# Attention and SwiGLU on one core: the first batch in groups of 128, 256 and 384 queries

## The chip, the cores and the metric

The kernel runs on one core of one Trainium2 chip. The metric is device time in microseconds of one execution, input loads and output stores included. TensorE (PE in the profile) multiplies matrices and turns tiles; VectorE (DVE) and ScalarE (ACT) work on elements; GpSimd (POOL) issues the loads that cast from float32 to bfloat16 and computes one small power for each group; SyncE (SP) issues the other DMAs. Each engine takes its instructions in the order of the program and waits for others through semaphores.

## The reference

Sparse attention over 4 batches, 8 heads, 768 positions and head dimension 64, then, over the 3072 rows of 512, a root-mean-square normalisation and a feed-forward block with gate:

```python
scores = scale * np.matmul(q, k.transpose(0, 1, 3, 2))
scores = np.where(mask, scores, -1e9)   # 32-wide blocks: neighbours, first, last, three sampled
attn = softmax(scores)
x = (attn @ v) as rows of H * D = 512
xn = x / np.sqrt(np.mean(x * x, axis=-1) + 1e-6) * rms_g
g, val = xn @ w_gate, xn @ w_val        # 512 -> 1536
out = (g * sigmoid(g) * val) @ w_out    # 1536 -> 512
```

## The kernel before

The work goes in groups of queries of one batch. `groups` (L51) holds three groups of 256 queries for batch 0 and two of 384 for each of the other three batches, nine in all. The main loop (L545) goes over the groups and inside over the eight heads. For a head, `scores` multiplies K (stationary, 128 keys at a time) with the group's queries into a PSUM tile `st` and ACT takes the exponential into `ex` (768 elements a partition in one instruction); the mask is carried by 24 extra rows of `KT` and `QT` below the 64 of the head, so that K, Q and mask are one product. One head later `pv` multiplies `ex` with V into the PSUM tile `op` (one buffer), and VectorE normalises it into `stage`.

The feed-forward of a group runs inside the attention of the next one. After the last head's `pv`, `after_pv` sums the squares on VectorE, POOL raises them to -0.5 (`rms_power`, L330, the tile `rstd`), VectorE scales the rows (`rms_scale`, the tile `xs`), and x is turned into `xg`: by TensorE and VectorE for the first two groups and the last (`transpose_x`), by a DMA transpose on SP for the others (`by_dma`, L335). At head `tx` of the next group `enter` (L438) puts the feed-forward's pieces into the list `fill`: a gate and a value product for each of 12 column blocks, then four parts of the down product for each 128 queries. `position` (L443) is called four times a head and emits pieces at the rate set by `enter`. So the order on each engine is written out by the loop, while the places of buffers in a pool are chosen when the program is built.

K and Q must be turned so that the head dimension lies on partitions. Batch 0's are turned by TensorE (`first_turn`, `transpose_qk`) and copied to `KT` and `QT` while the first group runs; the later batches' are turned by DMA transposes on SP (`turn`) and placed by further DMAs (`place`). `keep_busy` issues matmuls on zeros that nobody reads, in the first group (`thin`).

POOL issues in this order: the loads of batch 0 (K, Q and V by pairs of heads), the first half of the columns of the gate and value weights (`load_gv(0)`), in the first group's second head the other half and the down weights `wo`, then the first group's power, then in the second group K, Q and V of batch 1 for pairs 0 and 1, `gain`, K and Q of pairs 2 and 3, then the second group's power. Eight semaphores serve the loads in turn, so a load waits until the eighth one ahead of it has landed. SP issues, among others, the copies of the mask rows: for batch 1's buffers (`KT[1]`, `QT[1]`, 288 KB each) in the first group's sixth head (L478).

Of the kernel before, what the change touches and what calls it, by code (L numbers as in the profile page):

```python
# [17 lines left out]
def kernel(  # L18
# [18 lines left out]
    P = 128  # L37
# [10 lines left out]
    HC = NC // 2  # L48
    TGM = HC * P

    groups = [(0, c, 2) for c in range(0, NC, 2)]  # L51
    groups += [(b, c, HC) for b in range(1, B) for c in range(0, NC, HC)]
    FIRST = NC // 2
    KR = D + NB
    NP = H // 2
    VW = D + 1
# [30 lines left out]
    wg = persist.tile([P, KD, DFF], BF16, name="wg")  # L87
    wv = persist.tile([P, KD, DFF], BF16, name="wv")
    wo = persist.tile([P, NF, DM], BF16, name="wo")
    NWC = 2  # L90
    WC = DFF // NWC

    def load_gv(j):
        for t, src in ((wg, moe_w_gate), (wv, moe_w_val)):
            nc.gpsimd.dma_start(
                out=t[:, :, j * WC:(j + 1) * WC],
                in_=src.rearrange("(c p) f -> p c f", p=P)[:, :, j * WC:(j + 1) * WC])
# [5 lines left out]
    def cast_v(b, pr, eng):  # L103
        eng.tensor_copy(  # L104
            out=Vp[b % 2][:, 2 * pr:2 * pr + 2, :, 0:D], in_=vraw.pop((b, pr)))


# [55 lines left out]
    for pr in range(NP):  # L163
        if pr + 1 < NP:
            load_qk(0, pr + 1)
        load_v(0, pr)
    load_gv(0)

    mhalf = const.tile([P, HC], FP32, name="mhalf")
    nc.vector.memset(mhalf, -0.5)  # L170
# [79 lines left out]
    def transpose_qk(pr, which, lo, hi, spare, copy):  # L250

        b = 0
        src = (kbf if which == 0 else qbf)[(b, pr)]
        dst = (KT if which == 0 else QT)[b % 2]
        pool, tag = (ps_f, "ff") if spare else (ps_o, "ot")
        t = pool.tile([P, 2, HC, P], BF16, name="tqk", tag=tag)
        for e in range(2):
            for cc in range(lo, hi):  # L260
                nc.tensor.transpose(  # L261
                    out=t[:, e, cc, :], in_=src[:, e, 2 * cc * D:(2 * cc + 2) * D],
                    identity=ident)
        view = dst[0:D, 2 * pr:2 * pr + 2, :].rearrange("p e (c w s) -> p e c w s", w=2, s=P)
        for w in range(2):
            copy(out=view[:, :, lo:hi, w, :], in_=t[w * D:(w + 1) * D, :, lo:hi])  # L266

    turned = {}

# [19 lines left out]
    def scores(grp, h, part, ex):  # L289

        b, c0, n = grp
        tg = n * P
        nj = 2 if n == HC else 3
        st = ps_s.tile([P, 1024], FP32, name="st", tag="st")
        at = st.rearrange("p (j t) -> p j t", t=512 if n == HC else tg)
        for e in range(nj):
            jt = nj * part + e
            nc.tensor.matmul(  # L298
                out=at[:, e, 0:tg], lhsT=KT[b % 2][0:KR, h, jt * P:(jt + 1) * P],
                rhs=QT[b % 2][0:KR, h, c0 * P:c0 * P + tg], start=True, stop=True)  # L300
# [32 lines left out]
        e["xg"] = work.tile([P, KD, TGM], BF16, name="xg", tag="xg", bufs=2)  # L333

    def by_dma(e):  # L335
        return e["grp"] not in (groups[0], groups[1], groups[-1])

    def rms_scale(e, it):
        if it >= e["grp"][2]:
# [121 lines left out]
    def side_work(gi, h):  # L461

        if gi == 0:
            if h == 0:
                copy_rows(KT, kind, 2, 4, 0, S)
                copy_rows(QT, qmask, 2, 4, 0, 2 * P)
            if h % 2 == 0:
                cast_v(0, h // 2, nc.vector)
            if h == 1:
                load_gv(1)  # L470
                nc.gpsimd.dma_start(out=wo, in_=moe_w_out.rearrange("(c p) f -> p c f", p=P))
            if h == 1:
                for third in range(1, FIRST):
                    mask_queries(third)
                nc.sync.dma_start(
                    out=QT[0][D:KR, 1:H, 2 * P:S],
                    in_=qmask[:, 2 * P:S].unsqueeze(1).to_broadcast([NB, H - 1, S - 2 * P]))
            if h == 5:  # L478
                for T, m in ((KT, kind), (QT, qmask)):
                    nc.sync.dma_start(out=T[1][D:KR, :, :],  # L480
                                      in_=m.unsqueeze(1).to_broadcast([NB, H, S]))
        if gi == 1:
            if h == 1:
                load_qk(1, 0)
                load_v(1, 0)
                load_v(1, 1)
                load_qk(1, 1)
            if h == 3:
                nc.gpsimd.dma_start(
                    out=gain, in_=moe_rms_g.unsqueeze(0).to_broadcast([P, DM]))  # L490
                load_qk(1, 2)
            if h == 5:
                load_qk(1, 3)

    def turn_first(gi, h):


        if gi == 0 and h == 0:
            transpose_qk(1, 0, 0, HC, True, nc.vector.tensor_copy)
        if gi == 0 and 0 < h < H - 2:  # L500
            if h % 2:
                transpose_qk(h // 2 + 1, 1, 0, 1, True,
                             nc.scalar.copy if h < 4 else nc.vector.tensor_copy)
            else:
                transpose_qk(h // 2 + 1, 0, 0, HC, True, nc.vector.tensor_copy)
        if gi == 0 and h >= H - 2:
            e = h - (H - 2)
            t = first_turn((q16, second16[1])[e], 1, HC)
            for w in range(2):
                first_copy(e, 1, t, w, 1, HC, nc.vector.tensor_copy)  # L510
        if gi == 1 and h in (0, 2, 4):
            transpose_qk(h // 2 + 1, 1, 1, HC, h == 0, nc.vector.tensor_copy)

    def casts(gi, b, g, h):


        if gi + 1 < FIRST or h not in (2, 4):
            return
        n = h // 2 - 1
        if b == 0:  # L520
            cast_v(1, n, nc.vector)
            load_v(1, 2 + n)
            return
        if g == 0:
            cast_v(b, 2 + n, nc.vector)
        elif b + 1 < B:
            cast_v(b + 1, n, nc.vector)
        if b + 1 < B:
            load_v(b + 1, 2 * g + n)
            load_qk(b + 1, 2 * g + n)  # L530
# [13 lines left out]

    for gi, grp in enumerate(groups):  # L545
        b, c0, n = grp
        g = c0 // n
        parts = 3 if n == HC else 2
        cur = {
            "stage": work.tile([P, HC, DM], BF16, name="stage", tag="stage", bufs=2),  # L550
            "ssq": work.tile([P, HC], FP32, name="ssq", tag="ssq", bufs=2),
            "grp": grp,
        }
        tx = 1 if gi == 1 else TX
        for h in range(H):
            ex = ex_tile(n)
            thin = gi == 0 or (gi == 1 and h <= tx)
            if gi == 0 and h in (1, 2):
                keep_busy(2, 512)
            scores(grp, h, 0, ex)  # L560
            if h == 0 and prev is not None and prev[0]["grp"][2] == HC:
                squares(prev[0], 2, 0, (H - 1) * D)
            if gi == 0 and h == 0:
                scores(grp, h, 1, ex)
                second = [first_turn(t16, 0, 1 if which else HC)
                          for which, t16 in enumerate(second16)]
                for which in range(2):
                    for w in range(2):
                        first_copy(1, which, second[which], w, 0, 1 if which else HC,
                                   nc.vector.tensor_copy)  # L570
                copy_rows(KT, kind, 1, 2, 0, S)
                copy_rows(QT, qmask, 1, 2, 0, 2 * P)
                nc.vector.tensor_scalar(out=rmsg, in0=rmsg, scalar1=float(DM) ** 0.5,
                                        scalar2=None, op0=ALU.mult)
            if h == 1 and ending is not None and tx > 1:
                rms_scale(ending, 1)
            if h == tx and ending is not None and tx > 1:
                transpose_x(ending, 0)
            if gi == 0 and h:
                turn_first(gi, h)  # L580
            if thin:
                keep_busy(1, 512)
            position()
            if gi or h:
                scores(grp, h, 1, ex)
            side_work(gi, h)
            position()
            if h == 1 and ending is not None and tx > 1:
                rms_scale(ending, 2)
            if thin:  # L590
                keep_busy(1, 512)
# [9 lines left out]
            if h == tx == 1 and ending is not None:  # L601
                transpose_x(ending, 0)
# [6 lines left out]
            if h == tx and ending is not None:  # L609
                transpose_x(ending, 1)  # L610
                enter(ending, NPOS + 4 * (TX - tx))
                ending = None
            if gi == 1:
                turn_first(gi, h)
            casts(gi, b, g, h)
            turns(gi, b, g, h)
            if gi == FIRST and h == 0:
                nc.vector.tensor_scalar(out=gain, in0=gain, scalar1=float(DM) ** 0.5,
                                        scalar2=None, op0=ALU.mult)
            if h == 0 and ending is not None:  # L620
                rms_scale(ending, 0)
                if tx == 1:
                    rms_scale(ending, 1)
            if h == H - 1:
                squares(cur, 1, 0, (H - 1) * D)
            prev = (cur, h, ex)
    pe, ph, pex = prev
# [50 lines left out]
```

## Time and profile before

| | |
|---|---|
| median of 3 runs (lowest, highest) | 316.9 us (315.94, 317.04) |
| the profiled execution: its time, its span | 317.69 us, 315.9 us |
| TensorE matmul busy | 305.8 us, 97% of the span |
| TensorE weight load busy | 200.5 us |
| VectorE busy | 205.5 us |
| ScalarE busy | 207.4 us |
| GpSimd busy | 47.3 us |
| DMA moved | 37.24 MB, 118 GB/s over the span |

Durations of single instructions come from one profiled execution. Matmuls overlap, so the time that one costs in a row is the distance of starts and not the mean duration in its row. A row such as "rstd waits, idle 1.58 <-DVE ssq" says how long the engine had nothing to do before the instruction and what ended that. The landing time of a DMA is counted from its issue.

### The profile page before, as it was taken

How to read it: one execution, taken by the hardware profiler on the slowest of the kernel's cores; microseconds unless marked ns; L12 is line 12 of the kernel's file. 1: busy time of each engine (PE TensorE's matmuls, PEld its weight loads, DVE VectorE, ACT ScalarE, POOL GpSimd, SP SyncE). 2: the span in 40 equal slices, each digit the busy share in tenths (PEclk: the TensorE clock that was granted, in tenths of full speed). 3: DMA queues.
4: the chain of work that ended last, by engine and by line, in shares of the span. 5: the costliest groups of instructions: out<-in, count | busy, mean ns of one | idle time of the engine just before them, and what ended most of it. 6: DMA issues, size and time to landing. Idle time of an engine off the chain costs nothing.

```text
span 315.9 us, 7285 instructions
## 1 busy us (share of the span) xinstructions
PE 305.8 (97%) x2869; PEld 200.5 (63%) x2869; DVE 205.5 (65%) x563; ACT 207.4 (66%) x336; POOL 47.3 (15%) x70
## 2 busy tenths in 40 slices
PE   8888999999899999999999999999999999989995
PEld 4566886886588556655666566655666566645653
DVE  7987875678367657682767457683767546683860
ACT  6687776677688676676766766766767666722331
POOL 9705221000220122012020122010000100010000
PEclk9999999999999999999999999999999999999999
DMA  7999999997779487705784288814000230002002
GB/s 143 297 242 212 209 247 188 162 201 131 190 134 164 86 183 152 133 20 130 160 163 100 50 192 125 152 38 118 33 2 0 48 105 2 3 0 100 2 0 101
DMA packets 66766, 37.24 MB, mean 118 GB/s; under 512 B 49532, under 2 KB 62444, under 8 KB 66732
## 3 DMA queue, kind: packets, MB, share of 16 engines
q1 hardware_dynamic: 53000, 19.59, 29.2%
q0 software_dynamic: 13696, 17.17, 28.6%
q8 instruction: 22, 0.36, 0.5%
q14 instruction: 12, 0.10, 0.1%
q10 hardware_dynamic: 36, 0.01, 0.0%
HBM read 28.59 MB, written 6.29 MB: 110 GB/s over the span
## 4 chain that ended last, share of the span: by engine, by line
PE 89%; DVE 7%; DMA 2%; ACT 1%; issue 1%; POOL 0%; DVEq 0%; ACTq 0%
PE gp L379 20%; PE vp L390 19%; PE st L298 19%; PE yp L407 18%; PE op L310 11%; DVE junk L322 2%; DMA xg<-xs 2%; PE unread L151 1%; PE tx L361 1%; DVE stage L315 1%; ACT ex L301 1%; DVE KT L208 0%; DVE u L394 0%; PE tqk L261 0%; DVE KT L266 0%
## 5 line engine op out<-in xcount | busy, mean ns | idle before, releaser
L301 ACT ACTIVATE ex<-st 128x768 bf16<-128x768 f32 x192 | 154.4, 812 | 58.1 <-PE st L298 56.0
L298 PE MATMUL st<-QT,KT 88*128 88x384 bf16 (+1 forms) x432 | 94.6, 309 | 0.8 <-ACT ex L301 0.4
L394 DVE SCALAR_TENSOR_TENSOR u<-th,gp 128x384 bf16<-128x384 bf16 (+1 forms) x108 | 54.8, 508 | 43.1 <-ACT th L383 41.5
L379 PE MATMUL gp<-xg,wg 128*128 128x384 bf16 (+1 forms) x432 | 80.4, 307 | 1.2 <-DMA xg<-xs 1.2
L390 PE MATMUL vp<-xg,wv 128*128 128x384 bf16 (+1 forms) x432 | 80.1, 307 | 0.4 <-DVE u L394 0.4
L407 PE MATMUL yp<-wo,hps 128*128 128x512 bf16 (+1 forms) x300 | 74.0, 370 | 0.7 <-DVE hps L396 0.7
L383 ACT ACTIVATE th<-gp 128x384 bf16<-128x384 f32 (+1 forms) x108 | 48.9, 453 | 28.0 <-PE gp L379 27.8
L396 DVE TENSOR_TENSOR hps<-u,vp 128x384 bf16<-128x384 bf16 (+1 forms) x108 | 55.1, 510 | 11.7 <-PE st L298 0.5
L298 PEld LDWEIGHTS <-KT 88*128 88x128 bf16 x432 | 41.6, 98 | 26.9 <-DVE QT L222 1.3
L379 PEld LDWEIGHTS <-wg 128*128 128x128 bf16 x432 | 40.2, 97 | 21.9 <-DMA xg<-xs 1.3
L390 PEld LDWEIGHTS <-wv 128*128 128x128 bf16 x432 | 40.5, 97 | 20.8 <-issue 0.8
L310 PEld LDWEIGHTS <-ex 128*128 128x128 bf16 x1152 | 46.1, 98 | 11.5 <-DVE stage L315 1.3
L310 PE MATMUL op<-Vp,ex 128*128 128x65 bf16 x1152 | 48.8, 194 | 1.1 <-DVE stage L315 0.6
L407 PEld LDWEIGHTS <-hps 128*128 128x128 bf16 x300 | 27.7, 97 | 23.7 <-DVE hps L396 1.2
L314 DVE RECIPROCAL rz<-op 128x3 f32<-128x3 f32 (+1 forms) x72 | 12.5, 173 | 29.0 <-PE op L310 28.8
L330 POOL TENSOR_TENSOR rstd<-ssq,mhalf 128x3 f32<-128x3 f32 (+1 forms) x9 | 7.3, 814 | 150.0 <-DVE ssq L322 150.0
L315 DVE TENSOR_TENSOR stage<-op,rz 128x192 bf16<-128x192 f32 (+1 forms) x72 | 24.1, 335 | 2.5
L413 ACT ACTIVATE yo<-yp 128x512 f32<-128x512 f32 (+1 forms) x25 | 14.4, 577 | 17.0 <-PE yp L407 17.0
L83 POOL DMA_DIRECT2D vraw<-in_v_dram x16 | 12.0, 748 | 70.9 <-DVE Vp L104 70.7
L322 DVE CUSTOM_DVE_ANT_0 junk<-stage 128x448 bf16<-128x448 bf16 x24 | 14.9, 623 | 0.6
L342 DVE SCALAR_TENSOR_TENSOR xs<-stage,rstd,gain 128x512 bf16<-128x512 bf16 x17 | 11.8, 748 | 4.5 <-POOL rstd L330 4.4
L151 PE MATMUL unread<-idle 128*128 128x512 bf16 (+1 forms) x37 | 12.6, 391 | 1.2 <-DVE idle L144 1.2
(61 smaller groups left out, 98.7 us busy)
## 6 DMA issues: line engine op xcount, KB each, us to landing
vraw<-in_v_dram POOLq DMA_DIRECT2D x16, 384.0 KB, 4.9
out_dram<-yo SPq DMA_DIRECT2D x23, 256.0 KB, 2.3
kbf<-in_k_dram POOLq DMA_DIRECT2D x15, 192.0 KB, 6.2
qbf<-in_q_dram POOLq DMA_DIRECT2D x15, 192.0 KB, 6.5
KT<-turned SPq DMA_DIRECT2D x24, 96.0 KB, 3.6
QT<-turned SPq DMA_DIRECT2D x24, 96.0 KB, 2.4
wg<-in_moe_w_gate_dram POOLq DMA_DIRECT2D x2, 768.0 KB, 16.4
wv<-in_moe_w_val_dram POOLq DMA_DIRECT2D x2, 768.0 KB, 20.2
```

The costliest lines, as they stand in the source:

```text
L151: nc.tensor.matmul(out=t[:, 0:cols], lhsT=idle[:, 0:P], rhs=idle[:, 0:cols], start=True, stop=True)
L298: nc.tensor.matmul(out=at[:, e, 0:tg], lhsT=KT[b % 2][0:KR, h, jt * P:(jt + 1) * P], rhs=QT[b % 2][0:KR, h, c0 * P:c0 * P + tg], start=Tru ...
L301: nc.scalar.activation(out=ex[:, nj * part:nj * (part + 1), :], in_=at[:, 0:nj, 0:tg], func=AF.Exp, scale=SCALE)
L310: nc.tensor.matmul(out=op[:, it, 0:VW], lhsT=ex[:, jt, it * P:(it + 1) * P], rhs=Vp[b % 2][:, h, jt, :], start=(jt == 0), stop=(jt == NC - 1))
L315: nc.vector.tensor_tensor(out=stage[:, 0:n, h * D:(h + 1) * D], in0=op[:, 0:n, 0:D], in1=rz[:, 0:n].unsqueeze(2).to_broadcast([P, n, D]), ...
L322: nc.vector.tensor_tensor_reduce(out=junk[:, 0:hi - lo], in0=part, in1=part, scale=1.0, scalar=(e["ssq"][:, it:it + 1] if lo else DM * 1e- ...
L379: nc.tensor.matmul(out=gp[:, 0:tg], lhsT=wg[:, c, f * P:(f + 1) * P], rhs=xg[:, c, 0:tg], start=(c == 0), stop=(c == KD - 1))
L383: nc.scalar.activation(out=th[:, 0:tg], in_=gp[:, 0:tg], func=AF.Tanh, scale=0.5)
L390: nc.tensor.matmul(out=vp[:, 0:tg], lhsT=wv[:, c, f * P:(f + 1) * P], rhs=xg[:, c, 0:tg], start=(c == 0), stop=(c == KD - 1))
L394: nc.vector.scalar_tensor_tensor(out=u[:, 0:tg], in0=th[:, 0:tg], scalar=1.0, in1=gp[:, 0:tg], op0=ALU.add, op1=ALU.mult)
L396: nc.vector.tensor_tensor(out=hps[:, f, 0:tg], in0=u[:, 0:tg], in1=vp[:, 0:tg], op=ALU.mult)
L407: nc.tensor.matmul(out=yp, lhsT=hps[:, f, tt * P:(tt + 1) * P], rhs=wo[:, f, lo:hi], start=(f == 0), stop=(f == NF - 1))
```

## The change

Batch 0 goes in groups of 128, 256 and 384 queries, in this order. The number of groups stays nine. For 128 queries one `scores` call takes all six key blocks of a head (`nj` 6), so that there is one exponential a head in the first group, two in the second, three in the third. The third group's x is turned by TensorE instead of by DMA transposes. The weights' columns are loaded as a quarter and a quarter ahead of the main loop and a half in the first group's second head; `wo` follows as before. Half of the K copies and two V casts of batch 0 go to ACT, the Q copies to VectorE. The copies of the mask rows for batch 1 are issued by POOL in the second group's sixth head, behind K and Q of the last pair, instead of by SP in the first group. The second group's x enters at the third head for all groups.

```diff
-    groups = [(0, c, 2) for c in range(0, NC, 2)]
+    groups = [(0, 0, 1), (0, 1, 2), (0, 3, HC)]
     groups += [(b, c, HC) for b in range(1, B) for c in range(0, NC, HC)]
-    FIRST = NC // 2
+    FIRST = len(groups) - 2 * (B - 1)
...
-    load_gv(0)
+    load_gv(0, NF // 4)
+    load_gv(NF // 4, NF // 2)
...
-            copy(out=view[:, :, lo:hi, w, :], in_=t[w * D:(w + 1) * D, :, lo:hi])
+            copy[w](out=view[:, :, lo:hi, w, :], in_=t[w * D:(w + 1) * D, :, lo:hi])
...
-        nj = 2 if n == HC else 3
+        nj = {1: 6, 2: 3, 3: 2}[n]
...
-        return e["grp"] not in (groups[0], groups[1], groups[-1])
+        return e["grp"] not in groups[:FIRST] and e["grp"] != groups[-1]
...
-                cast_v(0, h // 2, nc.vector)
+                cast_v(0, h // 2, nc.vector.tensor_copy if h < 4 else nc.scalar.copy)
             if h == 1:
-                load_gv(1)
+                load_gv(NF // 2, NF)
...
-                    out=QT[0][D:KR, 1:H, 2 * P:S],
-                    in_=qmask[:, 2 * P:S].unsqueeze(1).to_broadcast([NB, H - 1, S - 2 * P]))
-            if h == 5:
-                for T, m in ((KT, kind), (QT, qmask)):
-                    nc.sync.dma_start(out=T[1][D:KR, :, :],
-                                      in_=m.unsqueeze(1).to_broadcast([NB, H, S]))
+                    out=QT[0][D:KR, 1:H, HC * P:S],
+                    in_=qmask[:, HC * P:S].unsqueeze(1).to_broadcast([NB, H - 1, S - HC * P]))
+            if h == 4:
+                copy_rows(QT, qmask, 1, H, 2 * P, HC * P)
         if gi == 1:
...
             if h == 5:
                 load_qk(1, 3)
+                for T, m in ((KT, kind), (QT, qmask)):
+                    nc.gpsimd.dma_start(out=T[1][D:KR, :, :],
+                                        in_=m.unsqueeze(1).to_broadcast([NB, H, S]))
...
-        tx = 1 if gi == 1 else TX
...
-            if h == tx and ending is not None and tx > 1:
+            if h == TX and ending is not None:
                 transpose_x(ending, 0)
+                if gi == 1:
+                    transpose_x(ending, 1)
+                    enter(ending, NPOS + 4)
+                    ending = None
```

In the built program after the change, POOL's instructions from the down weights on stand in this order, with what each waits for (the pairs of heads are counted from 0):

```
wo                     waits: V of batch 0, pair 2, landed
rstd, first group      waits: VectorE's squares
K(1,0) Q(1,0) V(1,0) V(1,1) K(1,1) Q(1,1) gain
K(1,2)                 waits: wo landed
Q(1,2)                 waits: K(1,0) landed
K(1,3)                 waits: Q(1,0) landed
Q(1,3)                 waits: V(1,0) landed, and SP's turn of Q(1,0) complete
mask rows of KT[1]     waits: V(1,1) landed
mask rows of QT[1]     waits: K(1,1) landed
rstd, second group     waits: VectorE's squares
```

In the program before, Q(1,3) has the buffer of batch 0's last Q pair and waits for TensorE's reading of that one; after the change it has the buffer of Q(1,0).

More of the change, by code (lines that the diff above doesn't have):

```diff
@@ L89, with load_gv @@
     wo = persist.tile([P, NF, DM], BF16, name="wo")
-    NWC = 2
-    WC = DFF // NWC
-    def load_gv(j):
+    def load_gv(lo, hi):
         for t, src in ((wg, moe_w_gate), (wv, moe_w_val)):
             nc.gpsimd.dma_start(
-                out=t[:, :, j * WC:(j + 1) * WC],
-                in_=src.rearrange("(c p) f -> p c f", p=P)[:, :, j * WC:(j + 1) * WC])
+                out=t[:, :, lo * P:hi * P],
+                in_=src.rearrange("(c p) f -> p c f", p=P)[:, :, lo * P:hi * P])
     KT = [persist.tile([P, H, S], BF16, name=f"KT{i}") for i in range(2)]
@@ L101, with cast_v @@
     Vp = [persist.tile([P, H, NC, VW], BF16, name=f"Vp{i}") for i in range(2)]
-    def cast_v(b, pr, eng):
-        eng.tensor_copy(
+    def cast_v(b, pr, copy=nc.vector.tensor_copy):
+        copy(
             out=Vp[b % 2][:, 2 * pr:2 * pr + 2, :, 0:D], in_=vraw.pop((b, pr)))
@@ L493, in side_work @@
                 load_qk(1, 3)
+                for T, m in ((KT, kind), (QT, qmask)):
+                    nc.gpsimd.dma_start(out=T[1][D:KR, :, :],
+                                        in_=m.unsqueeze(1).to_broadcast([NB, H, S]))
     def turn_first(gi, h):
+        dve, act = nc.vector.tensor_copy, nc.scalar.copy
         if gi == 0 and h == 0:
-            transpose_qk(1, 0, 0, HC, True, nc.vector.tensor_copy)
+            transpose_qk(1, 0, 0, HC, True, (dve, act))
         if gi == 0 and 0 < h < H - 2:
             if h % 2:
-                transpose_qk(h // 2 + 1, 1, 0, 1, True,
-                             nc.scalar.copy if h < 4 else nc.vector.tensor_copy)
+                transpose_qk(h // 2 + 1, 1, 0, 1, True, (dve, dve))
             else:
-                transpose_qk(h // 2 + 1, 0, 0, HC, True, nc.vector.tensor_copy)
+                transpose_qk(h // 2 + 1, 0, 0, HC, True, (dve, act))
         if gi == 0 and h >= H - 2:
@@ L511, in turn_first @@
         if gi == 1 and h in (0, 2, 4):
[L512 removed]
+            transpose_qk(h // 2 + 1, 1, 1, HC, h == 0, (dve, dve))
     def casts(gi, b, g, h):
@@ L520, in casts @@
         if b == 0:
-            cast_v(1, n, nc.vector)
+            cast_v(1, n)
             load_v(1, 2 + n)
@@ L524, in casts @@
         if g == 0:
-            cast_v(b, 2 + n, nc.vector)
+            cast_v(b, 2 + n)
         elif b + 1 < B:
-            cast_v(b + 1, n, nc.vector)
+            cast_v(b + 1, n)
         if b + 1 < B:
@@ L546 @@
         b, c0, n = grp
-        g = c0 // n
-        parts = 3 if n == HC else 2
+        g = 0 if c0 == 0 else 1
+        parts = n
         cur = {
@@ L553 @@
         }
-        tx = 1 if gi == 1 else TX
         for h in range(H):
             ex = ex_tile(n)
-            thin = gi == 0 or (gi == 1 and h <= tx)
+            thin = gi == 0 or (gi == 1 and h <= TX)
             if gi == 0 and h in (1, 2):
@@ L563 @@
             if gi == 0 and h == 0:
-                scores(grp, h, 1, ex)
                 second = [first_turn(t16, 0, 1 if which else HC)
                           for which, t16 in enumerate(second16)]
+                copy_rows(KT, kind, 1, 2, 0, S)
+                copy_rows(QT, qmask, 1, 2, 0, 2 * P)
                 for which in range(2):
@@ L569 @@
                         first_copy(1, which, second[which], w, 0, 1 if which else HC,
[L570 to L575, printed above, removed]
+                                   nc.vector.tensor_copy if which or not w else nc.scalar.copy)
+            if h == 1 and ending is not None:
                 rms_scale(ending, 1)
-            if h == tx and ending is not None and tx > 1:
+            if h == TX and ending is not None:
                 transpose_x(ending, 0)
+                if gi == 1:
+                    transpose_x(ending, 1)
+                    enter(ending, NPOS + 4)
+                    ending = None
             if gi == 0 and h:
@@ L583 @@
             position()
-            if gi or h:
+            if parts > 1:
                 scores(grp, h, 1, ex)
@@ L587 @@
             position()
-            if h == 1 and ending is not None and tx > 1:
+            if h == 1 and ending is not None:
                 rms_scale(ending, 2)
@@ L600 @@
                 copy_rows(QT, qmask, 4, H, 0, 2 * P)
-            if h == tx == 1 and ending is not None:
-                transpose_x(ending, 0)
             position()
@@ L608 @@
             position()
-            if h == tx and ending is not None:
+            if h == TX and ending is not None:
                 transpose_x(ending, 1)
-                enter(ending, NPOS + 4 * (TX - tx))
+                enter(ending, NPOS)
                 ending = None
@@ L616 @@
             turns(gi, b, g, h)
+            if gi == 0 and h == H - 1:
+                nc.vector.tensor_scalar(out=rmsg, in0=rmsg, scalar1=float(DM) ** 0.5,
+                                        scalar2=None, op0=ALU.mult)
             if gi == FIRST and h == 0:
@@ L621 @@
                 rms_scale(ending, 0)
-                if tx == 1:
-                    rms_scale(ending, 1)
-            if h == H - 1:
+            if h == H - 1 and n > 1:
                 squares(cur, 1, 0, (H - 1) * D)
```

## The prediction

> **What bounds it now.** I read the page's busy slices first, then the chain of waits, then the timelines of POOL and SP, because the change touches what those two issue.
>
> ```profile
> PE   8888999999899999999999999999999999989995
> ...
> DMA  7999999997779487705784288814000230002002
> ```
>
> TensorE is busy from the first slice to the last, so the time is its work plus what it can't do in the first microseconds and in waits. DMA is full over the first nine slices (71 us), while the weights and two batches load.
>
> ```profile
> 27.61 0.73 POOL rstd L330
> ...
> 28.37 0.78 DVE xs L348 x2
> ...
> 81.12 2.44 DMA xg<-xs
> 83.56 0.05 issue
> 83.60 0.61 PE gp L379 x4
> ```
>
> This is the chain: after the last head of a group it goes through POOL's power (rstd), VectorE's xs and, for the third group, a DMA transpose. On TensorE's timeline that transpose leaves 0.91 us idle, not 2.44.
>
> ```profile
> 14.71 1.03 POOL L471 DMA_DIRECT2D wo<-in_moe_w_out_dram  x1
> 27.61 0.72 POOL L330 TENSOR_TENSOR rstd<-ssq,mhalf 128x2 f32<-128x2 f32 x1 [11.87 <-DVE ssq L322]
> ...
> 44.31 0.70 POOL L75 DMA_DIRECT2D kbf<-in_k_dram  x1 [6.96 <-DMA wo<-in_moe_w_out_dram]
> 45.55 0.71 POOL L75 DMA_DIRECT2D qbf<-in_q_dram  x1 [0.54 <-PE op L310]
> 46.34 0.72 POOL L75 DMA_DIRECT2D kbf<-in_k_dram  x1
> 47.54 0.71 POOL L75 DMA_DIRECT2D qbf<-in_q_dram  x1 [0.49 <-PE vp L390]
> 49.83 0.71 POOL L330 TENSOR_TENSOR rstd<-ssq,mhalf 128x2 f32<-128x2 f32 x1 [1.58 <-DVE ssq L322]
> ```
>
> POOL works in order, and each load waits until the eighth load ahead of it has landed. The load at 44.31 waited 6.96 us for wo, which landed at 14.71 + 29.3 = 44.0. The second group's rstd stands behind these loads; at 49.83 POOL waited for it by 1.58 us only. That is all the slack there is.
>
> ```profile
> 14.41 0.78 SPq L480 DMA_DIRECT2D KT<-KT  x1
> 15.23 0.78 SPq L480 DMA_DIRECT2D QT<-QT  x1
> 45.08 1.32 SPq L274 DMA_TRANSPOSE turned<-kbf  x1
> ...
> 53.75 2.15 SPq L274 DMA_TRANSPOSE turned<-qbf  x1
> ```
>
> SP turns batch 1's first K as soon as it has landed (45.08). The view of DMA issues gives 9.4 us until that turn landed, against 2.8 to 3.2 us (median) after 84 us, when the queues are light.
>
> **The change, part by part.**
>
> *Work of TensorE.* Score matmuls start 0.109 us apart at 256 columns (three in 0.33) and 0.163 at 384, so they cost by the column; 128 wide I take 0.055, as the six transposes between 13.40 and 13.74. All products have as many columns as before, so the sum stays. Scores 62.6, gate and value 125.3, pv 37.1 (32 ns each), down 62.2: 287 of the 315.9 us. Third group by TensorE: 12 transposes x 0.056 = +0.7 against 0.9 idle: nothing.
>
> *First group.* It runs from 6.3 to 27.5 now, and VectorE is the pace (3.2 to 3.9 of every 4 us busy from 8 to 28). After: its instructions from 8.6 on, priced by their rows, are 8 x (0.165 + 0.225) normalisations, 3 x 0.55 K copies (the other halves go to ACT), 10 Q copies 2.85, 2 casts 1.4, row copies and masks 3.0, squares 0.7: 12.7 us, plus about 1 us of latency. It ends near 22.5, 5 us earlier, and leaves out 128 queries of attention, 8 x (0.33 + 0.19) = 4.2 us, to be done later. Real gain: about 1 us. ACT takes over three K half copies of about 0.81, two V casts and a copy; with eight exps that is some 11 us in 16, so it hides them (if not: the last rival). V for heads 4 to 7 lands at 16.4 and 17.4, in time.
>
> *Second group.* Per head 2 exps (1.62) and 1.5 tanh (0.27, from 489, 381 and the step between) make ACT 2.05 us against TensorE's 1.75; I take 2.2. It ends at 22.5 + 8 x 2.2 = 40. Then its rstd is wanted, 9 us earlier than now. The quarter loads cost nothing that TensorE sees: wg's first half now lands at 22.6, wv's at 29.2, and quarters land before the first gate, near 27.
>
> *Small edits.* The later turning of the second group's x (third head instead of second), fewer keep-busy matmuls and the moved rmsg product lie beside the work above or, for the second group, inside the wait below: nothing.
>
> *POOL's line.* All queue bytes up to batch 1's loads are the same, and DMA is full from 4 us on, so landings move only by the mask copies that leave SP. They and the shorter QT copy take away 0.615 MB, at 210 GB/s 2.9 us. So wo lands at 41.1, batch 1's first K at 42.1, q at 43.1, the two v at 44.1 and 45.1, the second k at 45.9. In the built program three things stand ahead of the second group's rstd that weren't there or were free: q of the last pair now takes the buffer of q of the first pair, so it waits until SP's turn of that one is complete; the K mask copy waits for the second v, the Q mask copy for the second k.
>
> The Trainium skill ("DMA: Bandwidth & Descriptors", Issuing engines are not separate DMA queues) says that DMAs of all issuing engines run on the same 16 engines and that moving them saves only issue time. By it the move buys no bandwidth; here it puts issue time on the engine that has none to give.
>
> *When that turn is complete.* In the built program q's turn follows K's on SP without the output of the first group between them (at 53.28 now): K at 42.1, q right behind. The first needed 9.4 us in this trace; by the packets of the hardware queue:
>
> ```profile
> q0 software_dynamic: 305, 0.36, 80.9%
> q1 hardware_dynamic: 200, 0.05, 45.0%
> ```
>
> (48 to 50 us; columns: packets, MB, share.) From 46 to 54 it got 82, 200, 327 and 191 packets in each 2 us, about 105 per us once going, and 2180 in 56 to 60 when the loads were done, 545 per us. One turn is 768 packets of 256 B, two 1536. From 44.5 to the end of the loads at 53.5: 945; the other 591 take 1.1 us: complete at 54.6. Bounds: both at the light rate, 46.5; both at 9.4 us, 60.9.
>
> *The wait.* Then POOL issues q, K mask, Q mask and computes rstd, 4 x 0.74 = 3.0: 57.6; xs 0.77: TensorE turns x of the second group at 58.4 instead of about 44. Behind the waiting xs on VectorE stand the last gate products of group one and the normalisation of the third group's first head; so TensorE can do two heads of scores and one pv, then has no work, because `op` has one buffer.
>
> *From there to the end.* Third group's eight heads of scores 7.8 and pv 4.6, first group's down 2.6, the second group's feed-forward 96 x 0.109 + 24 x 0.216 = 15.7, transposes 1.1: 31.8. The same kinds of work took 54.4 us for a listed 50.8 between 29.2 and 83.6 in this trace, so 31.8 x 1.07 = 34.0. From 83.6 the trace needs 315.9 - 83.6 = 232.3, plus 128 more queries in the third feed-forward, 96 x 0.054 + 12 x 0.216 = 7.8: 240.1. Sum: 58.4 + 34.0 + 240.1 = 332.5.
>
> *The clock after the gap.* At the start, before it has worked long, TensorE is slow:
>
> ```profile
> 4.68 1.70 PE L151 MATMUL unread<-idle 128*128 128x256 bf16 x7
> ...
> 10.07 0.50 PE L298 MATMUL st<-QT,KT 88*128 88x256 bf16 x3 [0.32 <-DVE QT L222]
> ```
>
> The seven start 0.22 us apart, the three 0.11: half rate until about 6.5, 5.4 us after its first matmul. The trace of before has no gap above 1.0 us after that, so a gap's cost is bounded by 0 and 2.7; I take 1.3, the middle. Span 333.8. The Trainium skill ("TensorE: Matmul & The Clock Gate", Part 1) says the clock halves after about 3.4 us of idleness and returns after as long of work; the 14 us gap would then cost 1.7 and the span be 334.2.
>
> The profiled execution took 317.69, 1.8 more than its span; the median is 0.8 less. So 333.8 + 1.0 = 334.8.
>
> **The rivals.**
>
> *The turns don't lag.* If both turns run near the light rate, the mask copies end the wait: second k at 45.9, Q mask 0.75, rstd 0.72, xs 0.77: TensorE goes on at 48.2, and the end is 48.2 + 34.0 + 240.1 + 1.0 = 323.3. For it: a turn alone takes 3 us. Against: the first took 9.4 in this very stretch.
>
> *Faster: POOL is clear in time.* Place: rstd of the second group at 40. It decides if the loads and turns ahead of it are complete by about 40 instead of 54.6. Then group one ends at 21.5, eight heads at ACT's 2.05 and two of the third group at 2.6 bring TensorE to the x transposes at 43.1, with the down products done: 43.1 + 28.6 x 1.07 + 240.1 = 313.8, 314.8 with the 1.0. Against it is the DMA row full up to there. A milder form, with heads at 2.2 and group one ending at 22.5 (45.3), gives 317.0: no change.
>
> *The first stage doesn't shorten.* If copies moved to ACT wait for its exps, group one ends as late as 26. The second group then ends near 44, still before 54.6: no change to the forecast, which the loads set.
>
> **How the numbers follow.** POOL's wait with lagging turns has 0.70, the one without 0.20, faster 0.05, no change 0.05. Turns at 60.9 with the full 2.7 give 342.5; 323 takes in the other slow case. Range 322 to 342. Under 0.5% (1.6 us, about what the measurement of this kernel can tell from no change) 0.05, slower 0.90, faster 0.05.
>
> **What would show it.** Right: POOL's issue of the last q after 50, its idle time before it named for SP's turn; rstd of the second group near 57; TensorE idle some 10 to 14 us around 45 to 58, ended by xs; busy as now from the fourth group on. The first group's x transposes near 23.5 would show the first stage right. Wrong: rstd of the second group before 45, or TensorE idle under 3 us there; then the loads were faster than their bytes say, or the second group slower than 2.2 us a head.

## The result, and the profile after

The changed kernel takes 335.49 us (median of 6 runs, 334.11 to 335.85), the kernel before, timed beside it, 316.94 us (315.94 to 317.12): the ratio is 1.0585, with an interval of 1.0558 to 1.0611. It is 18.6 us slower. The profiled execution took 335.81 us, its span is 334.0 us. The forecast was 334.8 us, with a span of 333.8. A few executions of one kernel run longer at a lower granted clock (one of 18 of the kernel before took 321.35 us at 0.995, the others at most 317.88 at 0.998 or more); the ratios leave such runs out, the medians don't.

The busy slices of the page of the changed kernel (8.35 us each; its line numbers lie one or two below those of the kernel before):

```profile
span 334.0 us, 7290 instructions
...
PE   7799900999999999999999999999999999999996
...
PEclk9999975699999999999999999999999999999999
DMA  7999999299247726784479436761400040001002
```

Slices 6 and 7 (42 to 58 us) are empty on TensorE; from slice 8 on it is as busy as before. The clock falls in the same place. POOL's timeline (start, duration, instruction; in brackets the idle time ahead of it and what ended that):

```profile
24.00 0.58 POOL L329 TENSOR_TENSOR rstd<-ssq,mhalf 128x1 f32<-128x1 f32 x1 [6.18 <-DVE ssq L321]
...
41.41 0.71 POOL L75 DMA_DIRECT2D kbf<-in_k_dram  x1 [6.96 <-DMA wo<-in_moe_w_out_dram]
42.64 0.72 POOL L75 DMA_DIRECT2D qbf<-in_q_dram  x1 [0.53 <-PE op L309]
43.44 0.72 POOL L75 DMA_DIRECT2D kbf<-in_k_dram  x1
53.99 0.72 POOL L75 DMA_DIRECT2D qbf<-in_q_dram  x1 [9.84 <-DMA turned<-qbf]
54.70 0.68 POOL L492 DMA_DIRECT2D KT<-KT  x1
55.38 0.66 POOL L492 DMA_DIRECT2D QT<-QT  x1
56.05 0.73 POOL L329 TENSOR_TENSOR rstd<-ssq,mhalf 128x2 f32<-128x2 f32 x1
```

The last Q load of batch 1 stood 9.84 us for SP's turn of the first Q, whose buffer it takes. Behind it stood the two mask copies and the second group's power, whose squares were long done: its row names no wait of its own. SP's timeline, and then TensorE's, show the two ends of that:

```profile
42.16 1.32 SPq L273 DMA_TRANSPOSE turned<-kbf  x1
43.61 2.50 SPq L273 DMA_TRANSPOSE turned<-qbf  x1
```

```profile
41.74 0.74 PE L309 MATMUL op<-Vp,ex 128*128 128x65 bf16 x18
57.68 0.58 PE L389 MATMUL vp<-xg,wv 128*128 128x128 bf16 x4 [15.20 <-DVE u L393]
58.05 1.48 PE L297 MATMUL st<-QT,KT 88*128 88x384 bf16 x4
59.34 0.63 PE L360 MATMUL tx<-ident,xs 128*128 128x128 bf16 x4
```

TensorE's wait is put down to VectorE's `u`; but `u` stood behind `xs` on VectorE, and the waits of this stretch (36 to 66 us; total, times, longest) say what `xs` waited for:

```profile
PE vp L389 <- DVE u L393: 15.5, 2, 15.2
DVE xs L347 <- POOL rstd L329: 15.3, 1, 15.3
POOL qbf L75 <- DMA turned<-qbf: 9.8, 1, 9.8
```

So the chain reads backwards: TensorE for VectorE's product, that for POOL's power, that for a load, that for a DMA turn. The third column from the right in these windows is the granted clock:

```profile
44.00:48.00 4.00, 0.00 (x0) 0.00 (x0) 0.00 (x0) 0.00 (x0) 0.15 (x1) 0.81 1.29 219
48.00:52.00 4.00, 0.00 (x0) 0.00 (x0) 0.00 (x0) 0.00 (x0) 0.00 (x0) 0.50 1.49 134
...
60.00:64.00 4.00, 3.78 (x26) 1.97 (x26) 0.61 (x2) 1.26 (x2) 0.00 (x0) 0.55 0.15 31
64.00:68.00 4.00, 4.00 (x43) 2.68 (x42) 2.15 (x7) 3.02 (x5) 0.76 (x1) 1.00 0.19 66
```

At half rate four score matmuls took 1.48 us at 58.05.

### The profile page after: what moved, and what is told of

Its sections match the earlier page's. It is cut to its first block, busy times and chain, and to the rows that moved or that the text cites. A ratio compares the mean times of both kernels' runs of the same rounds, so it can differ in the third digit from the quotient of the medians.

```text
span 334.0 us, 7290 instructions
## 1 busy us (share of the span) xinstructions
PE 308.2 (92%) x2862; PEld 196.6 (59%) x2879; DVE 203.1 (61%) x566; ACT 209.1 (63%) x338; POOL 50.1 (15%) x74
## 4 chain that ended last, share of the span: by engine, by line
PE 84%; DVE 5%; DMA 5%; ACT 2%; POOL 2%; issue 1%; SPq 0%; DVEq 0%; POOLq 0%
PE gp L378 18%; PE st L297 18%; PE vp L389 18%; PE yp L406 18%; PE op L309 10%; DMA turned<-qbf 3%; DMA vraw<-in_v_dram 2%; ACT ex L300 1%; DVE junk L321 1%; DVE u L393 1%; DVE hps L395 1%; PE tx L360 1%; DVE stage L314 1%; DVE QT L265 1%; PE unread L149 1%
## 5 line engine op out<-in xcount | busy, mean ns | idle before, releaser
L297 PE MATMUL st<-QT,KT 88*128 88x384 bf16 (+2 forms) x432 | 95.1, 310 | 2.7 <-DVE QT L265 0.9
L389 PE MATMUL vp<-xg,wv 128*128 128x384 bf16 (+2 forms) x432 | 80.4, 308 | 15.5 <-DVE u L393 15.5
L378 PE MATMUL gp<-xg,wg 128*128 128x384 bf16 (+2 forms) x432 | 80.8, 307 | 0.0
L393 DVE SCALAR_TENSOR_TENSOR u<-th,gp 128x384 bf16<-128x384 bf16 (+2 forms) x108 | 54.8, 508 | 42.1 <-ACT th L382 40.8
L406 PE MATMUL yp<-wo,hps 128*128 128x512 bf16 (+1 forms) x285 | 72.5, 374 | 0.9 <-issue 0.2
L382 ACT ACTIVATE th<-gp 128x384 bf16<-128x384 f32 (+2 forms) x108 | 49.0, 454 | 32.5 <-PE gp L378 32.4
L395 DVE TENSOR_TENSOR hps<-u,vp 128x384 bf16<-128x384 bf16 (+2 forms) x108 | 55.1, 510 | 11.3
L313 DVE RECIPROCAL rz<-op 128x3 f32<-128x3 f32 (+2 forms) x72 | 12.6, 174 | 32.6 <-PE op L309 32.3
L329 POOL TENSOR_TENSOR rstd<-ssq,mhalf 128x3 f32<-128x3 f32 (+2 forms) x9 | 7.6, 842 | 147.5 <-DVE ssq L321 147.5
L314 DVE TENSOR_TENSOR stage<-op,rz 128x192 bf16<-128x192 f32 (+2 forms) x72 | 24.1, 335 | 2.5
L149 PE MATMUL unread<-idle 128*128 128x512 bf16 (+1 forms) x37 | 11.8, 379 | 1.8 <-DVE idle L142 1.2
## 6 DMA issues: line engine op xcount, KB each, us to landing
wo<-in_moe_w_out_dram POOLq DMA_DIRECT2D x1, 1536.0 KB, 24.3
```

The source lines that it names most:

```text
L149: nc.tensor.matmul(out=t[:, 0:cols], lhsT=idle[:, 0:P], rhs=idle[:, 0:cols], start=True, stop=True)
L297: nc.tensor.matmul(out=at[:, e, 0:tg], lhsT=KT[b % 2][0:KR, h, jt * P:(jt + 1) * P], rhs=QT[b % 2][0:KR, h, c0 * P:c0 * P + tg], start=Tru ...
L314: nc.vector.tensor_tensor(out=stage[:, 0:n, h * D:(h + 1) * D], in0=op[:, 0:n, 0:D], in1=rz[:, 0:n].unsqueeze(2).to_broadcast([P, n, D]), ...
L378: nc.tensor.matmul(out=gp[:, 0:tg], lhsT=wg[:, c, f * P:(f + 1) * P], rhs=xg[:, c, 0:tg], start=(c == 0), stop=(c == KD - 1))
L382: nc.scalar.activation(out=th[:, 0:tg], in_=gp[:, 0:tg], func=AF.Tanh, scale=0.5)
L389: nc.tensor.matmul(out=vp[:, 0:tg], lhsT=wv[:, c, f * P:(f + 1) * P], rhs=xg[:, c, 0:tg], start=(c == 0), stop=(c == KD - 1))
```

## The experiments

Ten kernels ran. Four (e1 to e4) change one thing in the changed kernel; e5 makes one part of the change in the kernel before; the others ask what is late next once POOL's wait is gone. In the code, `...` marks lines left out. Each ratio is to the kernel before on the same chip (316.6 to 317.0 us).

**One more Q buffer (e1_qbf5).** The last Q load gets a buffer of its own. Room for it comes from letting the half-wide output tile share the full one's buffers.

```diff
-            t = ld.tile([P, 2, NC * D], BF16, name=name, tag=name, bufs=4)
+            t = ld.tile([P, 2, NC * D], BF16, name=name, tag=name, bufs=5 if name == "qbf" else 4)
...
-                yo = work.tile([P, hi - lo], FP32, name="yo", tag=f"yo{hi - lo}",
-                               bufs=3 if hi - lo == DM else 2)
+                yo = work.tile([P, DM], FP32, name="yo", tag="yo", bufs=3)[:, 0:hi - lo]
```

> The changed kernel with five buffers instead of four for the loaded Q (room made by letting the half-width output tile share the full one's buffers), so that the last Q pair of batch 1 no longer waits for SP's turn of the first pair. Theory (that turn holds POOL, 9.8 us): POOL issues the last Q near 44, the mask copies when the second V and the second K have landed (44.9 and 46.0), rstd of the second group near 46.7 instead of 56.05, TensorE goes on near 48.2 instead of 57.7; what remains is the wait of the mask copies, some 5 to 6 us. Time 335.5 - 9.5 = 326, or 325 if the clock falls less. Rival (the mask copies or the loads themselves hold POOL, the turn is only the last to come): no more than 1 us less, 334 to 336.

Measured: 326.51 us, ratio 1.032 (1.0282 to 1.0357). POOL's timeline:

```profile
44.77 0.72 POOL L75 DMA_DIRECT2D qbf<-in_q_dram  x1 [0.59 <-DMA vraw<-in_v_dram]
45.48 0.68 POOL L491 DMA_DIRECT2D KT<-KT  x1
46.29 0.66 POOL L491 DMA_DIRECT2D QT<-QT  x1
46.96 0.73 POOL L329 TENSOR_TENSOR rstd<-ssq,mhalf 128x2 f32<-128x2 f32 x1
```

The power comes 9.1 us earlier, and the time falls by 9.0: of the 9.84 us that POOL waited for the turn, 9 were on the path. What is left of the gap (6.49 us on TensorE, until 48.59) is the rest of POOL's line: its issue at 41.72 had to wait for `wo` (16.4 + 24.8 = 41.2), and behind it six issues of about 0.7 us, with about 1 us of short waits among them, stand ahead of the power.

**Mask copies back on SP (e2_masks_sp).** Issued by SP in the first group, as before; the buffer's wait stays.

```diff
+            if h == 5:
+                for T, m in ((KT, kind), (QT, qmask)):
+                    nc.sync.dma_start(out=T[1][D:KR, :, :],
+                                      in_=m.unsqueeze(1).to_broadcast([NB, H, S]))
...
                 load_qk(1, 3)
-                for T, m in ((KT, kind), (QT, qmask)):
-                    nc.gpsimd.dma_start(out=T[1][D:KR, :, :],
-                                        in_=m.unsqueeze(1).to_broadcast([NB, H, S]))
```

> The changed kernel with the mask rows of batch 1's buffers copied by SP in the first group's sixth head, as in the kernel before; the wait for the turn stays. Theory (the turn holds POOL): the loads land 2 to 3 us later because the mask copies use the DMA engines early, the turn is complete near 56, POOL saves two issues (1.35): 335 to 337, no gain. Rival (the mask copies on POOL are the cause): rstd of the second group is on time, 317 to 320.

Measured: 339.41 us, ratio 1.0719 (1.0691 to 1.0748): no gain, and 2.4 us above the range that was expected. POOL's timeline:

```profile
58.38 0.72 POOL L75 DMA_DIRECT2D qbf<-in_q_dram  x1 [10.32 <-DMA turned<-qbf]
59.12 0.73 POOL L329 TENSOR_TENSOR rstd<-ssq,mhalf 128x2 f32<-128x2 f32 x1
```

Two issues left POOL's line, but 0.59 MB went back into the stretch in which the weights load: POOL could issue behind `wo` at 45.43 instead of 41.41, and the power came 3.1 us later. So the mask copies on POOL are not the cause; where their move counts, it is as bytes taken out of the full stretch.

**Masks on POOL in the kernel before (e5_before_masks).** The same move the other way, alone, in the kernel before.

> The kernel before with one part of the change alone: the mask rows of batch 1's buffers copied by POOL in the second group's sixth head instead of by SP in the first group. In this built program the last Q pair keeps the buffer of batch 0's last pair, so POOL does not wait for SP's turn. Theory (the move costs only where POOL's line is short of slack and the turn stands in it): the loads land 2.5 to 3 us earlier, the last Q near 44.7, the mask copies when the second V and K are there (45 and 46), rstd of the second group at 49.8 as before; 316 to 318. Rival (mask copies behind the loads cost by themselves, by holding POOL or by crowding the later turns): 319 or more.

Measured: 317.4 us, ratio 1.0018 (1.0006 to 1.0029). POOL's timeline:

```profile
44.33 0.72 POOL L75 DMA_DIRECT2D qbf<-in_q_dram  x1 [0.56 <-PE gp L379]
45.04 0.68 POOL L491 DMA_DIRECT2D KT<-KT  x1
45.88 0.66 POOL L491 DMA_DIRECT2D QT<-QT  x1 [0.16 <-issue]
49.32 0.71 POOL L330 TENSOR_TENSOR rstd<-ssq,mhalf 128x2 f32<-128x2 f32 x1 [2.78 <-DVE ssq L322]
```

The last Q load waits 0.56 us, the two mask issues follow, and POOL still waits 2.78 us for the second group's squares. The same instructions cost less than 1 us where the group ends behind them.

**TensorE kept busy in the gap (e4_warm).** Sixty 512-wide matmuls on zeros fill most of it, so that only the clock changes.

```diff
                 if ph == H - 1:
                     ending = pe
+            if gi == 2 and h == 1:
+                gap = ps_s.tile([P, 1024], FP32, name="gap", tag="st")
+                keep_busy(60, 512, gap)
```

(The lines stand behind that head's `pv`.)

> The changed kernel with 60 matmuls on zeros, 512 columns each, put on TensorE right where its gap begins (they use a scores buffer that is free then); the wait itself stays. They last 13 us at full rate and end before the gap does. Theory (after the gap TensorE runs at half rate from 57.7 to 63.4, which costs half of that): the rows after the gap at full distance, 0.163 instead of 0.32 a score matmul, time 2.5 to 3 us less, 332.5 to 333. Rival (VectorE's and ScalarE's backlog paces those microseconds, not the clock): 334.5 to 336.

Measured: 333.43 us, ratio 1.055 (1.0508 to 1.0593), a granted clock of 1.0 over the whole profile. That is 0.4 us above the range that was expected, and its runs (332.69 to 334.95) touch those of the changed kernel (334.11 to 335.85). TensorE's timeline:

```profile
42.39 13.11 PE L149 MATMUL gap<-idle 128*128 128x512 bf16 x60
57.36 0.38 PE L389 MATMUL vp<-xg,wv 128*128 128x128 bf16 x4 [1.86 <-DVE u L393]
57.58 0.82 PE L297 MATMUL st<-QT,KT 88*128 88x384 bf16 x4
```

The four score matmuls take 0.82 us instead of 1.48. The half clock costs 2.1 us by the medians, 3.1 by the two spans; 0.3 of the latter is POOL's power, which came at 55.73 in this profile.

**Late loads (e3_late_pool).** K and Q of pairs 2 and 3 and the masks move behind the second group's power on POOL.

```diff
-                load_qk(1, 2)
-            if h == 5:
-                load_qk(1, 3)
-                for T, m in ((KT, kind), (QT, qmask)):
-                    nc.gpsimd.dma_start(out=T[1][D:KR, :, :],
...
+        if gi == 2 and h == 1:
+            load_qk(1, 2)
+            load_qk(1, 3)
+            for T, m in ((KT, kind), (QT, qmask)):
+                nc.gpsimd.dma_start(out=T[1][D:KR, :, :],
...
```

> The changed kernel with the loads of K and Q of pairs 2 and 3 of batch 1 and the mask copies issued by POOL after the second group's power (in the third group's second head) instead of before it. Theory (all that is lost is POOL's line ahead of the second group's power): rstd of the second group at about 39.6, as soon as the squares are there, TensorE without a gap over 1 us there, and the end where the prediction's rival without a wait puts it: 314 to 318 us. Rival (groups of 128 and 256 cost by themselves: short matmuls, ScalarE's pace): 320 or more. Other rival (the late loads make batch 1 late): a gap at the start of the fourth group, 318 to 322.

Measured: 328.58 us, ratio 1.0225 (1.0115 to 1.0335). Its runs spread from 321.26 to 332.67; the ratio rests on two of them, 321.26 and 326.02, and the profile is of the longest, so the stall below has its size from that one. POOL's and TensorE's timelines:

```profile
41.55 0.72 POOL L329 TENSOR_TENSOR rstd<-ssq,mhalf 128x2 f32<-128x2 f32 x1 [7.01 <-DVE ssq L321]
```

```profile
76.70 0.80 PE L297 MATMUL st<-QT,KT 88*128 88x384 bf16 x2 [11.30 <-DMA QT<-turned]
```

The power comes as soon as the squares are there, and the third group has no gap over 0.9 us. But TensorE now stands still at the start of the fourth group, and the DMA issues (54 to 76 us; the last column is the median time to landing) show why:

```profile
vraw<-in_v_dram POOLq DMA_DIRECT2D x2, 384.0 KB, 18.2
...
KT<-KT POOLq DMA_DIRECT2D x1, 288.0 KB, 11.4
QT<-QT POOLq DMA_DIRECT2D x1, 288.0 KB, 17.0
```

The moved loads, the masks, V and the turns now meet at 54 to 76 us. The expectation of 314 to 318 took the batch's data to be early enough; in this execution it wasn't, and the rival with the gap at the fourth group was right in kind. The run of 321.26 had a granted clock of 1.0, against 0.979 in the one profiled, so it probably had no such gap, which no trace shows; even so it is 3 us above the range.

**Late loads, masks early on SP (e7_late_sp).** As above, with the masks issued by SP in the first group.

> The changed kernel with both: the loads of K and Q of pairs 2 and 3 of batch 1 behind the second group's power on POOL, and the mask rows copied by SP in the first group, as before the change. Theory (in the run with late loads and late mask copies, TensorE was on time in the third group and then waited 11.3 us for batch 1's first turned Q, because two turns, the mask copies and two V loads shared the DMA engines from 54 to 76): with the masks out of the way batch 1's first pair is placed by 60 to 64, later pairs every 7 us, TensorE needs them from 66 on every 9 us; no wait over 2 us; 315 to 319 us. Rival (the turns and placings on SP are the next bound whatever the masks do): a gap of 5 us or more at the fourth group's start, 321 or more.

Measured: 324.16 us, ratio 1.0234 (1.0217 to 1.0251). No gap at the fourth group, so neither theory holds as written (the rival's 321 or more is met, but not by its gap): the loss is elsewhere. The masks' bytes delay the value weights (TensorE's timeline):

```profile
37.45 0.60 PE L389 MATMUL vp<-xg,wv 128*128 128x128 bf16 x4 [1.83 <-DMA wv<-in_moe_w_val_dram]
```

The second group's power then comes at 45.62, not 41.55, and the third group's at 74.36. The latter is about where the kernel before stands (74.97), which then has 128 queries of feed-forward fewer left. That explains most of the loss (the sum stands at the end of the next section), and the expectation should have counted it: no time is won unless the third group ends earlier than before by the work that it holds over.

**Weights in halves (e8_halves).** As e7_late_sp, with `load_gv(0, NF // 2)` in place of the two quarters.

> The kernel of the run with late loads and early masks (both orders changed), with the gate and value weights loaded in halves as before the change instead of a quarter, a quarter and a half. Theory (the quarters only serve the first group's early feed-forward): the first gate product at 26 finds its half (landed near 23 to 24), the first value product at 27 waits for the value half until 28 to 30; 0 to 3 us more than with quarters. Rival (the prediction's words that quarters cost and bring nothing): within 0.5 us.

Measured: 323.19 us, ratio 1.0195 (1.0174 to 1.0215), about 1 us less instead of 0 to 3 more. The first value product waits 0.88 us for its weights and the fourth group 1.7 us for its first Q, but the second half of the weights no longer is late (e7's 1.83 us), and the second group's power comes at 42.86. The quarter loads bring nothing here.

**Third group's x by DMA again (e9_xdma).** As e7_late_sp, with `groups[:2]` in place of `groups[:FIRST]` in `by_dma`.

> The kernel of the run with late loads and early masks, with the third group's x turned by DMA as before the change. Theory (the prediction's 0.7 against 0.9 us): within 1 us of the same kernel with TensorE's turning. Rival (the DMA engines and SP's line are crowded there by the turns of batch 1, so that x comes late): 2 us more or worse.

Measured: 335.91 us, ratio 1.0593 (1.0555 to 1.0631): 11.8 us more, far from the expected 1. SP's timeline and the waits (20 to 100 us):

```profile
81.85 1.26 SPq L282 DMA_DIRECT2D QT<-turned  x2
83.21 4.44 SPq L344 DMA_TRANSPOSE xg<-xs  x3
```

```profile
PE gp L378 <- DMA xg<-xs: 10.1, 1, 10.1
```

x was ready for SP by about 78 (power at 74.96 for 1.08 us, then three xs of 0.75), but SP turns and places batch 1 until 83. TensorE then waits 10.1 us and goes on at half clock (0.50 over 92 to 96 us). So having TensorE turn x is worth some 12 us here, not the 0.2 that its own duration and the wait of before suggested. That holds in e7; in the changed kernel itself, where the third group's power comes 13 us later (87.46), it wasn't tried.

**Masks by VectorE (e10_dve_masks), and batch 1's first pair ahead of `wo` (e11_early_first).** Both start from e8_halves. The first part below is in both and stands in place of the mask DMAs; the second is in e11 alone, where `load_qk(1, 0)` also leaves the second group.

```diff
+        if gi == 2:
+            T, m = ((KT, kind), (QT, qmask))[h % 2]
+            nc.vector.tensor_copy(
+                out=T[1][D:KR, 2 * (h // 2):2 * (h // 2) + 2, :],
+                in_=m.unsqueeze(1).to_broadcast([NB, 2, S]))
...
                 load_gv(NF // 2, NF)
+                load_qk(1, 0)
```

> This is the kernel with the late batch 1 loads and half-and-half weights (e8_halves), with the mask rows of KT[1] and QT[1] written by VectorE in eight copies in the third group's heads instead of by two DMAs on SP. Theory (the early landings of the weights are what is short): 0.59 MB leave the queues before 40 us, at 210 GB/s 2.8 us, so the first value product doesn't wait (0.88 us in e8_halves), wo and batch 1 land some 2.5 us earlier, the wait of 1.71 us at the fourth group goes, and the time is 1.5 to 4 us under e8_halves' 323.2: 319 to 321.7. Rival (VectorE sets the pace of the third group, each copy some 0.5 us on the path): within 1 us of e8_halves or above it. Rival (a version faster than before): under 315, which needs the third group's rstd by about 67 us (72.48 in e8_halves).

> As e10_dve_masks, and the loads of batch 1's first K and Q stand ahead of the down weights wo. Theory (the late start of SP's turns holds the batch 1 chain): the first turn starts some 7 us earlier, near 35 us, wo lands 2 us later, near 43, in time for the first down product; the last Q of batch 1 waits less; the time is 0.5 to 2 us under e10_dve_masks, 318 to 321. Rival (the chain wasn't late any more, or the turns take bandwidth from the weights): equal to e10_dve_masks within 0.5 us, or up to 2 us slower by a wait for wo.

Measured: e10 321.59 us, ratio 1.0154 (1.0134 to 1.0174); e11 320.99 us, ratio 1.015 (1.0115 to 1.0185). Both times lie near the upper end of what the theories gave. Their waits are gone, the weights' and the fourth group's, and SP's first turn starts at 41.92 and at 34.00 (44.86 in e8). But by the ratios e10 is 1.3 us under e8, not 1.5 to 4, close to the rival's bound of 1; and between e10 and e11 the intervals overlap, so the 0.6 us there isn't shown. These are the best versions found with these groups, and they are still slower than the kernel before. What is left shows on TensorE's timeline of e11:

```profile
39.08 0.38 PE L388 MATMUL vp<-xg,wv 128*128 128x128 bf16 x4 [0.35 <-DVE u L392]
...
40.90 0.38 PE L388 MATMUL vp<-xg,wv 128*128 128x128 bf16 x4 [0.17 <-DVE u L392]
...
44.16 0.38 PE L388 MATMUL vp<-xg,wv 128*128 128x128 bf16 x4 [1.57 <-DVE u L392]
...
45.72 0.40 PE L359 MATMUL tx<-ident,xs 128*128 128x128 bf16 x4 [0.53 <-DVE stage L313]
```

These waits come to 2.6 us, and e11's span is 2.4 us above that of the kernel before (318.3 and 315.9). They stand at the end of the second group, where squares, power, xs, the last gate products of the first group and now a mask copy of 0.55 us follow each other on VectorE. No run takes them away, but TensorE's busy time from 30 to 55 us, in the kernel before and then in e11, agrees (behind the window stand its length and TensorE's busy time):

```profile
30.00:55.00 25.00, 24.59 (x286) 19.99 (x285) 18.08 (x59) 18.28 (x31) 6.83 (x10) 1.00 1.22 215
30.00:55.00 25.00, 22.10 (x289) 16.83 (x288) 18.49 (x63) 19.07 (x36) 5.37 (x8) 1.00 1.17 209
```

TensorE is idle there 2.9 us in e11 and 0.4 before. In the first 30 us it is idle 5.1 and 4.3 us, with the same number of matmuls on zeros (45) in both, and from 55 to 85 us 0.1 and 0.9. So the smaller first group, which was to shorten the first stage, took no idle time out of it.

## Why the prediction was right

The case that the forecast put first is what happened, and its steps can be laid beside the trace.

*Landings by their bytes.* `wo` was put at 41.1 and landed at 41.1 (issue at 16.79, 24.3 us to landing). Batch 1's first K was put at 42.1: SP began its turn at 42.16.

*The turn.* Complete at 54.6 by packets; measured 43.61 + 9.8 = 53.4. The bounds of 46.5 and 60.9 hold it well inside, and the rival in which the turns don't lag falls. e1, which comes nearest to it, took 326.5 and not 323.3: the power comes at 46.96, as that rival had it (46.65), but a gap of 6.5 us halves the clock too (0.50 over 44 to 52 us), and with a value product and scores at half rate ahead of them the x transposes come at 50.25 instead of 48.2.

*POOL's line.* Power computed by 57.6; measured 56.05 + 0.73 = 56.8, four instructions of about 0.7 us as said. e1 shows that the queue position is the mechanism, e5 that the move of the masks alone isn't.

*TensorE.* It was to stop with two heads of scores and one `pv` done; it stopped at 42.5 with one head, four of the second head's six score matmuls and that `pv` done, since a value product stood in between. So the gap was 15.2 us and not 10 to 14. The x transposes were put at 58.4 and came at 59.34: a value product and four score matmuls stood ahead of them, at half rate, and the sum hadn't counted those.

*From there to the end.* Transposes to the third group's first gate product: 34.0 without the clock. In e11, which has no gap, it is 79.36 - 45.72 = 33.6; in the changed kernel 95.10 - 59.34 = 35.8. From the gate product on: 240.1 in the sum, 334.0 - 95.10 = 238.9 measured, and the same 238.9 in e11 (318.3 - 79.36).

*The clock.* This is the term that was mis-sized: 1.3 us taken, with bounds of 0 and 2.7; the trace gives 2.1 behind the transposes (35.8 - 33.6) and 0.8 ahead of them (1.66 us from the value product to the transposes, 0.87 in e4). Together that is 2.9, just above the upper bound; by e4 the whole is 2.1 to 3.1. The bound itself was read too low from the start of the kernel before:

```profile
6.27 1.64 PE L298 MATMUL st<-QT,KT 88*128 88x256 bf16 x6
```

These six are still slow (372 to 421 ns each, against 272 to 283 for the three at 10.07), the last of them at 7.5. So the half rate lasted some 6.3 us there and not 5.4, which makes the upper bound 3.2.

*Luck in the sum.* The transposes came 0.9 late (POOL 0.8 early, the work ahead of them some 1.7 more), the next stretch was 0.5 longer than 34.0 + 1.3, and the last 1.2 shorter than 240.1: 0.9 + 0.5 - 1.2 = 0.2 us of span. So the path is the one that was forecast, but the agreement to 0.2 us is partly chance.

*The first group.* Its x transposes came at 25.08, not 23.5. TensorE waits there for ACT (the K copies and V casts moved to it, up to 0.42 us a time) and for VectorE's Q copies (up to 0.74), so ACT didn't hide its new work fully. As the last rival said, this changed nothing: the loads set the next step.

*What the sums at nothing were worth.* "Quarter loads cost nothing" and "third x by TensorE: nothing" weren't tried under the stall; the changed kernel's trace only shows no wait of TensorE for weights. With the stall gone, quarters cost 1 us against halves (e8), and TensorE's turning of the third x saves 12 (e9). The two rivals without POOL's wait, 314.8 and 317.0, were too cheap as well: the best version took 321.0, since the value weights, SP's turns and VectorE's chain were late next.

*What the idea has to reach.* The kernel before needs 232.3 us from the third group's first gate product on, the new grouping 238.9 to 239.7 in every run of it but e9 (240.8, half the clock at its start), as more queries are left to do. So that product must come before 315.9 - 238.9 = 77.0 us only to draw level. TensorE's timelines of the changed kernel and of e11:

```profile
95.10 0.99 PE L378 MATMUL gp<-xg,wg 128*128 128x384 bf16 x4
```

```profile
79.36 0.99 PE L377 MATMUL gp<-xg,wg 128*128 128x384 bf16 x4
```

In e7 it stands at 81.99. Of the 18.6 us that the change cost, 9.0 go with the one buffer (e1); the best version leaves 4.3 by the medians. If TensorE's whole idle time between 30 and 85 us in e11, 3.0 us, were gone, its span would be 315.3, an estimate from the busy times above: 0.6 us under the kernel before.

## What to carry to other kernels

Before moving an issue or a group's end, write out the in-order queue that the group's small but needed instruction stands in, with the wait of each entry in the built program: here a buffer choice that no line of the source shows put a 0.7 us power behind a 9.8 us DMA turn. A finished product that is due earlier needs all that stands ahead of it earlier too; and where the loads fill the DMA engines, they don't come earlier. For a regrouping, work out first by when the regrouped part must end to draw level with the old order, since work that it leaves for later is no gain.

## What the runs showed of the hardware

A DMA turn of 192 KB took 9.8 us from issue to landing beside full load queues, against medians of 2.8 to 3.2 from 84 us on in the kernel before. In e3 SP stood 9.84 us in issuing one, at 61.41, where the others up to there took 1.3 to 2.6. In 44 to 50 us of the changed kernel the hardware queue got 816 packets (0.20 MB) while the loads got 1034 (0.97 MB); that is 136 packets per us for the hardware queue, against 545 in the kernel before at 56 to 60 us, when the loads were done. The Trainium skill ("DMA: Bandwidth & Descriptors", Queues, rings and completion order) says that an engine takes turns between its queues packet by packet; the trace agrees in that both queues advance at the same time. Whether the profile's packets are those of the skill, and in what order they went, it doesn't show.

The clock: TensorE's last work ended at 42.5; a granted 0.81 over 44 to 48 (62% of the window at the full rate, the rest at half) puts the halving at 46.5, and 0.55 over 60 to 64 puts the return at 63.6, 5.9 us after work went on at 57.7. The Trainium skill ("TensorE: Matmul & The Clock Gate", Part 1) gives for each at least one window of about 3.4 us, and windows that run freely and don't start with the gap; the 4.0 and 5.9 here fit that. The cost of 2.1 to 3.1 us is more than the 1.7 that the prediction worked out from 3.4. In two places the clock halved after less idleness than one window: in e1 1.4 us into its gap of 6.49 us (0.94 over 40 to 44), and in e7 the windows around the wait of 1.83 us at 37.45 show 0.69 and 0.89 (36 to 40 and 40 to 44), with TensorE busy 2.55 us of the first four. What in those stretches counted as idle stays open.
